# S4 convolution and SwiGLU, two layers on one core: blocks 1 to 3 of layer 0 transformed during the kernel stage

## The chip, the cores and the metric

The kernel runs on one core of a Trainium2 chip. The metric is the device time of one execution in microseconds; a profile of one execution is read beside it. The engines are called PE (matrix multiply), DVE (vector), ACT (activations), POOL (GpSimd) and SP (which issues most transfers). The matrix results land in PSUM, everything else is in SBUF or in DRAM scratch tensors.

## What is computed

x has 2048 rows of 512 channels, and two layers follow each other. A layer first adds a long convolution of the normalised rows, with a kernel K of 2048 lags per channel that is built from a diagonal state space of 128 states, and then adds a SwiGLU feed-forward network (512 to 1376 and back).

```
x = x + S4(layernorm(x)); x = x + FFN(layernorm(x))      # twice, same weights
K[d,l]  = Re sum_n C[d,n] dt[d] B[d,n] exp(dt[d] A[d,n] l)
S4(u)   = irfft(rfft(u, 2L) * rfft(K, 2L))[:L] + u * Dskip
FFN(v)  = (silu(v @ w_gate) * (v @ w_up)) @ w_down
```

## The kernel before

The sequence is cut into four blocks of 512 rows. A block's normalised rows are transformed by products with DFT matrices into eight **units**, one for each half h of the channels and each q of four groups of frequencies; a unit is a tile u of 128 x 2 x 256. Block b's output needs the units of blocks 0 to b, each multiplied by a spectrum of the convolution kernel (w0r for lag block 0, wdr in DRAM for the others), and an inverse transform. Units that are used again are kept in DRAM, in udr.

**The kernel stage** (to about 290 us) builds K for 64 channels at a time, in eight chunks. Inside `tc.manual_schedule` the order of instructions on ACT, DVE and PE is the order in which the program writes them; the transfers on SP and the work on POOL are placed by a scheduler. In pass i of the loop DVE builds the powers for chunk i + 1 (`gen_g`, `gen_e`) and the turns for chunk i + 2 (`gen_turns`, whose first instruction, L349, opens DVE's pass); ACT computes exponentials (mu and re) and sines; PE multiplies them to lags (`lags`, pk), spreads them (`spread`, kp, which also adds d_skip from the tile dsk) and transforms them into spectra (`spectra`, pw). ACT squares the FFN weights on the way (L306, `norm_units`: three loads into buffers of tag "w", three squares, three PE products, twice in a pass) to find their scales.

Units come from two routines. `direct` (L271) makes a unit with eight fp32 products (L276), a copy from PSUM by ACT (L279) and a write to udr by SP (L280). `forward` (L230) makes the eight units of a block with additions on DVE (tiles bt and z, L216), a split into two fp16 halves by ACT and DVE, twelve fp16 products a unit (L260) and a copy by ACT (L262).

- Block 0 of layer 0: `direct`, eight units, before the loop.
- Block 1 of layer 0: its rows are normalised before the loop and written to ndr; `second` loads them (two loads of 256 KB a unit, tag "w") and makes one unit in each of passes 0 to 5, and two more behind the loop.
- Blocks 2 and 3 of layer 0, and blocks 0 to 3 of layer 1: `forward`, during the FFN stretch, after a load of the block's rows and their normalisation on ACT (`norm_x`).

A tag names a set of buffers: "w" has three, "t" and "y1" one. A tile takes the buffer of the tile before it, once that one's last reader is done. During the loop dsk lies in "t" and mz2 (the powers at the five doublings) in "y1".

**The FFN stretch** (from 345 us) alternates a block's convolution (`ssm`, mostly DVE: products L683 and sums L686, then fp16 inverse products L702 on PE) with the FFN of the block before it (`ffn`, mostly PE), in the order SEQ: layer 0's blocks 0, 1, 2, layer 1's block 0, layer 0's block 3, layer 1's blocks 1, 2, 3. A scheduler sets the order there. `inputs` hands the units out, one ahead of its use.

Of the kernel before, what the change touches and what calls it, by code (L numbers as in the profile page):

```python
# [11 lines left out]
F32 = mybir.dt.float32  # L12
# [24 lines left out]
NA = 21  # L37
TB = 256
BOOST = 1 << 20
HALF = 2  # L40
INV = 1
SEQ = ((0, 0), (0, 1), (0, 2), (1, 0), (0, 3), (1, 1), (1, 2), (1, 3))

# [29 lines left out]
def kernel(ctx, tc, x, a_re, a_im, b_re, b_im, c_re, c_im, log_dt, d_skip,  # L73
# [66 lines left out]
    G.memset(hpi, math.pi / 2)  # L140

    wdr = dram.tile([NB, 2, 4, P, 2, HD], F32, name="wdr")
    udr = [dram.tile([NB - 1, 2, 4, P, 2, HD], F32, name=f"udr{i}") for i in range(NL)]
    xdr = dram.tile([NB, 4, P, D], F32, name="xdr")
    ndr = dram.tile([2, 2, P, 2, HD], F32, name="ndr")


    e0, er_, ep = (sb.tile([P, 4], F32, name=f"e{i}") for i in range(3))
# [80 lines left out]
    def forward(n, h, eh):  # L229


        hs = slice(h * HD, (h + 1) * HD)
        x0, x1, x2, x3 = (n[:, c, hs] for c in range(4))
        bt = tl([P, 7, HD], "bt", "bt")
        a_, b_, p_, q_, r_, s_, hx = (bt[:, i] for i in range(7))
        stt(a_, x2, HH, x0, OP.add)
        stt(b_, x2, -HH, x0, OP.add)
        A.activation(hx, x2, AF.Copy, scale=HH)
        stt(p_, x3, TT, x1, OP.add)
        stt(r_, x3, -TT, x1, OP.add)  # L240
        stt(q_, x1, TT, x3, OP.subtract)
        stt(s_, x1, TT, x3, OP.add)
        for i, q in enumerate(QORD):
            z = z2[:, 0 if eh else i % 2]
# [3 lines left out]
            if eh:  # L248
                hl = z2[:, 1].bitcast(F16).rearrange("p i (l d) -> p l i d", l=2)
                A.activation(hl[:, 0], z, AF.Copy, scale=256.0)  # L250
                stt(hl[:, 1], z, 256.0, hl[:, 0], OP.subtract)
            pf = psml([P, 2, HD], "pf")
            with tc.high_priority(offset=BOOST):
                for o in range(2):
                    if eh:
                        terms = [(eh[:, q, o + i, le], hl[:, lz, i]) for i in range(2) for le, lz in ((0, 0), (0, 1), (1, 0))]
                    else:
                        terms = [(ef[:, q, o + i], z[:, i]) for i in range(2)]
                    for k, (e, m) in enumerate(terms):
                        PE.matmul(pf[:, o], lhsT=e, rhs=m, start=k == 0, stop=k == len(terms) - 1)  # L260
                u = tl([P, 2, HD], "u", "u")
                A.activation(u, pf, AF.Copy, scale=2.0 ** -16 if eh else 1.0)  # L262
            yield q, u

    def norm_early(xt, n, factors):
# [13 lines left out]
        A.activation(u, pf, AF.Copy)  # L279
        nc.sync.dma_start(udr[0][b, h, q], u)  # L280

    def second(h, q, space=psml):
        n = []
        for cp in range(2):
            t = tl([P, 2, HD], "n1", "w")
            nc.sync.dma_start(t, ndr[h, cp])
            n += [t[:, 0], t[:, 1]]
        return direct(1, h, q, n, space)


    def norms():
# [38 lines left out]
        V.tensor_scalar(sc6.bitcast(I32), bits, 23, None, OP.logical_shift_left)  # L330

    mz2 = tl([P, 2, 5, DC], "mz2", "y1")

    def gen_tiles(ch):
        re = tl([P, DC, 65], "re", f"W{2 * (ch % 2)}")
# [127 lines left out]
    def spread(ch, ks):  # L465


        kp = pbig([P, 4, 16, 16], "kp")
        for grp in range(4):
            d0 = ch * DC + 16 * grp  # L470
            for ga in range(4):
                PE.matmul(kp[32 * ga:32 * ga + 32, grp], lhsT=ident[:, 32 * grp:32 * grp + 32], rhs=ks[:, ga],
                          start=True, stop=ga > 0, tile_position=(0, 32 * ga))
            PE.matmul(kp[0:32, grp, 0], lhsT=ident[0:1, 0:32], rhs=dsk[:, d0:d0 + 16], start=False, stop=True,
                      tile_position=(0, 0))
        return kp

# [132 lines left out]

    def inputs():

        for layer, b in SEQ:
# [17 lines left out]
            if (layer, b) == SEQ[HALF]:  # L631
                eh.append(tl([P, 4, 3, 2, P], "eh", "ef", F16))
                nc.sync.dma_start(eh[0], c_eh)
            for h in range(2):
                for q, u in forward(n, h, eh[0] if eh else None):
# [210 lines left out]
    with tc.manual_schedule(engines={mybir.EngineType.Activation, mybir.EngineType.DVE, mybir.EngineType.PE}):  # L846
# [35 lines left out]
        take(fw[3], 1)  # L882
        for h in range(2):
            for cp in range(2):
                nc.sync.dma_start(ndr[h, cp], x1[:, 2 * cp:2 * cp + 2, h * HD:(h + 1) * HD])
        for f in fw[4:6]:
            take(tr, 1)
            take(f, 1)
# [5 lines left out]
        take(ex, 13)  # L894
        take(fw[7], 1)
        kt2 = tl([P, 2, 4, 16, 16], "kt2", "xf")
        sec = [(h, q) for h in range(2) for q in QORD]
        sp = iter(())
        for i in range(NCH - 1):
            pk = lags(ts[i], gs[i])  # L900
            more = i + 2 < NCH
            tn = rd = f = iter(())
            if more:
                ts[i + 2] = gen_tiles(i + 2)
                tn = gen_turns(i + 2, ts[i + 2])
            gs[i + 1] = tl([P, 2, DC, 32], "g", ("gb", "ga")[i % 2])
            gg, ge = gen_g(i + 1, ts[i + 1], gs[i + 1]), gen_e(ts[i + 1])
            take(ex, 100)
            take(sp, 2)
# [24 lines left out]
            while tops:  # L934
                tops.pop(0)()
            take(sp, 1)
            kp = spread(i, ks)
            if more:
                f = second(*sec[i])
                next(f)  # L940
            take(gg, 1)
            take(rd, 1)
            take(gg, 1)
            take(rd, 3)
            if more:
                tr = gen_trig(ts[i + 2])
                take(tr, 1)
            kt = kt2[:, i % 2]
            A.activation(kt, kp, AF.Copy)
            take(tr, 1)  # L950
            take(f, 1)
            take(tr, 1)
            take(gg, 1)
            if more:
                sp = spectra(i, kt, 0, NB)
                take(sp, 1)
                ex = gen_exp(i + 2, ts[i + 2])
                take(ex, 9)
                norm_units(3, 9)
                take(ex, 4)  # L960
                take(sp, 2)
                norm_units(0, 0)
                take(ex, 14)
                take(sp, 2)
                sizes(i, kt, ks)
                take(ge, 2)
                take(gg, 1)
                take(ge, 2)
                while tops:
                    tops.pop(0)()  # L970
                ts[i] = gs[i] = None
            else:
                sizes(i, kt, ks)
                take(ge, 2)
                take(gg, 1)
                take(ge, 2)
# [8 lines left out]
        xs, eh = [None] * 3, []  # L985
        spec, ahead = inputs(), []
        first = ssm(0, 0)
        sp = spectra(i, kt, 0, NB, QORD[:3])
# [45 lines left out]
        take(pscale, 1)  # L1034
        take(first, 2)
        take(rest, 2)
        take(second(*sec[-2], space=pbig), 2)
# [6 lines left out]
        take(second(*sec[-1], space=pbig), 2)  # L1044
        take(rest, 100)
        split(1, 0)
        take(first, 1)
# [48 lines left out]
```

## Time and profile before

| | us |
|---|---|
| median of 3 runs (1209.34 to 1214.46) | 1213.57 |
| the profiled execution, span | 1210.1 |
| PE busy | 1104.0 |
| DVE busy | 1048.5 |
| ACT busy | 646.3 |
| POOL busy | 187.8 |
| the passes of the loop, on DVE | 31.05, 33.86, 34.13, 33.87, 34.14, 32.92, 29.50 |
| end of the last pass to the first FFN matmul | 56.8 |
| FFN stretch, 345 us to the end | 865 |

A row of the view by stages gives a stretch, its length, and the busy time of each engine with its number of instructions; PEclk is the share of full clock that TensorE was granted. A row of the timeline gives start and length in us, engine, line, operation, output <- inputs, shapes and count, and in brackets the idle time of the engine before it and what ended it. A row of the view by lines ends with busy us, mean ns of one | idle time before. Shapes of matmuls are weights, then moving data; an fp32 product stands as two records. A row of transfers ends with KB each and the median us from issue to landing.

### The profile page before, as it was taken

The numbers are of one execution on the slowest core, as the hardware profiler recorded it, in microseconds if no ns is written. First come the engines' busy times: TensorE is split into PE (matmuls) and PEld (weight loads), VectorE is DVE, ScalarE is ACT, GpSimd is POOL, SyncE is SP. The second block draws the span as 40 slices with busy tenths as digits, with TensorE's granted clock in tenths as the row PEclk, the third lists the DMA queues.
The fourth block names the chain that finished last, engine by engine and source line by source line (L and its number), as shares of the span: only waits on it lengthen the run. The fifth ranks groups of instructions, "written<-read, shape, count | busy, mean of one in ns | idle before, by whom it ended". The sixth has DMA issues, their size and how long they took to land.

```text
span 1210.1 us, 25368 instructions
## 1 busy us (share of the span) xinstructions
PE 1104.0 (91%) x10220; PEld 858.5 (71%) x10220; DVE 1048.5 (87%) x1677; ACT 646.3 (53%) x1392; POOL 187.8 (16%) x209
## 2 busy tenths in 40 slices
PE   3877988888978998989999999999999999999998
PEld 2755766666976776868686777778686776867875
DVE  8999999999869999999998999999992799983221
ACT  7999999973265545526753524664431553324111
POOL 1116343453220010101100000121000010000000
PEclk9999998889999999999999999999999999999999
DMA  6223233236389427433245353424433144311000
GB/s 226 96 88 92 72 89 86 73 107 184 116 285 264 127 67 199 133 118 88 62 157 140 105 179 133 125 79 146 140 118 129 33 119 132 117 58 44 14 23 18
DMA packets 134857, 138.66 MB, mean 115 GB/s; under 512 B 75921, under 2 KB 85137, under 8 KB 134738
## 3 DMA queue, kind: packets, MB, share of 16 engines
q1 hardware_dynamic: 132178, 128.64, 35.4%
q0 software_dynamic: 2560, 8.39, 2.0%
q8 instruction: 80, 1.31, 0.5%
q14 instruction: 39, 0.32, 0.1%
HBM read 98.71 MB, written 28.31 MB: 105 GB/s over the span
## 4 chain that ended last, share of the span: by engine, by line
DVE 32%; PE 27%; issue 5%; DMA 4%; ACT 2%; POOL 2%; SPq 1%; DVEq 0%; ACTq 0%; POOLq 0%
DVE t L683 5%; PE pgu L807 5%; PE pgu L808 5%; PE pgu L809 5%; DVE yk L686 4%; DVE z L216 3%; DVE yk L683 3%; PE py L821 3%; PE py L822 3%; PE py L823 3%; PE pi L702 2%; DVE sg L813 2%; DVE hl L815 1%; DVE yl L216 1%; DVE bt L216 1%
## 5 line engine op out<-in xcount | busy, mean ns | idle before, releaser
L807 PE MATMUL pgu<-mix,wsl 128*128 128x256 f16 x1280 | 350.5, 274 | 7.9 <-DVE sg L813 4.4
L809 PE MATMUL pgu<-mix,wsl 128*128 128x256 f16 x1280 | 350.5, 274 | 1.2 <-DVE wsl L579 1.2
L808 PE MATMUL pgu<-mix,wsl 128*128 128x256 f16 x1280 | 350.4, 274 | 0.0
L808 PEld LDWEIGHTS <-wsl 128*128 128x128 f16 x1280 | 125.8, 98 | 24.6 <-issue 8.6
L821 PE MATMUL py<-wsl,hh 128*128 128x512 f16 (+1 forms) x352 | 134.6, 382 | 9.3 <-DVE xg L826 5.3
L809 PEld LDWEIGHTS <-wsl 128*128 128x128 f16 x1280 | 125.8, 98 | 16.5 <-DVE wsl L579 1.5
L807 PEld LDWEIGHTS <-wsl 128*128 128x128 f16 x1280 | 125.8, 98 | 15.8
L823 PE MATMUL py<-wsl,hl 128*128 128x512 f16 (+1 forms) x352 | 134.4, 382 | 2.4 <-DVE hl L815 2.4
L812 ACT ACTIVATE sg<-pgu,sc 128x512 f32<-128x512 f32 x80 | 54.5, 682 | 128.8 <-PE pgu L809 110.9
L822 PE MATMUL py<-wsl,hh 128*128 128x512 f16 x320 | 122.1, 382 | 0.0
L683 DVE TENSOR_TENSOR t<-uu,w 128x1024 f32<-128x1024 f32 x96 | 116.8, 1217 | 5.5 <-DMA uu<-udr 5.3
L686 DVE TENSOR_TENSOR yk<-yk,t 128x1024 f32<-128x1024 f32 x96 | 116.7, 1215 | 0.1
L493 PE MATMUL pw<-kt,ek 128*128 128x256 f32 (+2 forms) x420 | 105.4, 392 | 0.0
L813 DVE SCALAR_TENSOR_TENSOR sg<-pgu,sc,sg 128x512 f32<-128x512 f32 x80 | 59.6, 744 | 52.3 <-ACT sg L812 52.0
L702 PE MATMUL pi<-yl,mix 128*128 128x256 f16 x672 | 91.4, 273 | 5.5 <-ACT yl L691 3.5
L493 PEld LDWEIGHTS pw<-kt,ek 128*128 128x128 f32 x420 | 83.9, 208 | 11.9
L814 ACT ACTIVATE hh<-sg 128x512 f16<-128x512 f32 x80 | 50.0, 626 | 67.6 <-DVE sg L813 67.6
L211 POOL TENSOR_TENSOR rs<-mv,mhalf 128x2 f32<-128x2 f32 (+1 forms) x21 | 38.7, 1845 | 275.7 <-ACT mv L210 275.6
L260 PE MATMUL pf<-z,eh 128*128 128x256 f16 x576 | 74.4, 272 | 1.6 <-ACT z L250 1.6
L702 PEld LDWEIGHTS <-mix 128*128 128x128 f16 x672 | 65.3, 98 | 14.3 <-issue 3.9
L691 ACT ACTIVATE yl<-mix,sy 128x512 f16<-128x512 f32 x56 | 40.2, 717 | 61.4 <-DVE mix L688 61.2
L504 POOL COPY w0r<-s 128x128 f32<-128x128 f32 x29 | 48.1, 1659 | 141.7 <-ACT s L502 122.2
(221 smaller groups left out, 2292.0 us busy)
## 6 DMA issues: line engine op xcount, KB each, us to landing
w<-wdr SPq DMA_DIRECT2D x96, 256.0 KB, 2.8
uu<-udr SPq DMA_DIRECT2D x96, 256.0 KB, 3.0
udr<-u POOLq DMA_DIRECT2D x32, 256.0 KB, 2.8
wdr<-wo SPq DMA_DIRECT2D x96, 64.0 KB, 2.0
udr<-u SPq DMA_DIRECT2D x16, 256.0 KB, 2.5
n<-ndr SPq DMA_DIRECT2D x16, 256.0 KB, 3.0
n<-xdr SPq DMA_DIRECT2D x4, 1024.0 KB, 6.0
xg<-in_A_u_dram SPq DMA_DIRECT2D x3, 1024.0 KB, 7.4
```

What stands on the lines that cost most here:

```text
L260: PE.matmul(pf[:, o], lhsT=e, rhs=m, start=k == 0, stop=k == len(terms) - 1)
L493: PE.matmul(pw[:, i], lhsT=e, rhs=kt[:, :, c + 4 * k0:4 * k1:4, :].rearrange("p g k d -> p k g d"), start=c == 0, stop=c == 3)
L683: V.tensor_tensor(t, uu.unsqueeze(1).to_broadcast([P, 2, 2, HD]), w.unsqueeze(2).to_broadcast([P, 2, 2, HD]), OP.mult)
L686: V.tensor_tensor(yk, yk, t, OP.add)
L702: PE.matmul(pi[:, o], lhsT=e, rhs=m, start=k == 0, stop=k == len(terms) - 1)
L807: PE.matmul(o, lhsT=wgu(wi, k, 0)[:, fs], rhs=nh[:, k], start=k == 0, stop=False)
L808: PE.matmul(o, lhsT=wgu(wi, k, 0)[:, fs], rhs=nlo[:, k], start=False, stop=False)
L809: PE.matmul(o, lhsT=wgu(wi, k, 1)[:, fs], rhs=nh[:, k], start=False, stop=k == 3)
L813: V.scalar_tensor_tensor(sg, pgu[:, 1], sc6[:, 4:5], sg, OP.mult, OP.mult)
L821: PE.matmul(py[:, r], lhsT=hh[:n, f, rc], rhs=wd(f, 0)[:n], start=f == 0, stop=False)
L822: PE.matmul(py[:, r], lhsT=hh[:n, f, rc], rhs=wd(f, 1)[:n], start=False, stop=False)
L823: PE.matmul(py[:, r], lhsT=hl[:n, f, rc], rhs=wd(f, 0)[:n], start=False, stop=f == FT - 1)
```

## The change

Blocks 1 to 3 of layer 0 are now all made by `direct` during the kernel stage, 24 units instead of 8.

- `early_row(b, c)` loads 128 rows of x into a tile xr2 (tag "w"), takes bn_stats and bn_aggr on DVE, the reciprocal root on POOL (two operations), scales on DVE and writes to ndr. Blocks 2 and 3 have eight such rows; two are done in each of passes 0 to 3.
- `later()` hands out the 24 units in order. For each block and half it loads one tile n1 of 512 KB into tag "t", which four units read.
- A pass makes three units (fa behind the lags, f behind kp, fc between two spectra), the last pass four (fa, f and two more behind f); the last two follow behind the loop as before.
- `forward` keeps only its fp16 form, and layer 0 does not use it. `inputs` loads the units of layer 0's blocks from udr. That removes two blocks of `norm_x` and `forward` from the FFN stretch; 8 writes of units from POOL's queue go too.
- Since n1 takes "t", d_skip is loaded in two halves, into the end of a tile mzd that also holds mz2, and into wx.

```diff
-    dsk = tl([1, D], "dsk", "t")
-    nc.sync.dma_start(dsk, d_skip)
+    mzd = tl([P, 4 * HD], "mzd", "y1")
+    mz2 = mzd[:, :2 * 5 * DC].rearrange("p (k l d) -> p k l d", k=2, l=5)
+    dsk = mzd[0:1, 3 * HD:], wx.bitcast(F32)[0:1]
...
+    def early_row(b, c):
+
+        xr = tl([P, D], "xr2", "w")
+        nc.sync.dma_start(xr, x[0, b * T + c * P:b * T + (c + 1) * P, :])
+        row = tl([P, 16], "row", "stats")
+        st, mv, rs = row[:, :6], row[:, 6:8], row[:, 8:9]
+        V.bn_stats(st, xr)
+        V.bn_aggr(mv, st)
+        G.tensor_scalar(rs, mv[:, 1:2], EPS, 1.0, OP.add, OP.mult)
+        G.tensor_tensor(rs, rs, mhalf[:, 0:1], OP.pow)
+        yield
+        V.tensor_scalar(xr, xr, mv[:, 0:1], rs, OP.subtract, OP.mult)
+        nc.sync.dma_start(ndr[b - 1, :, :, c].rearrange("h p d -> p h d"), xr.rearrange("p (h d) -> p h d", h=2))
+
+    def later():
+
+        for b in range(1, NB):
+            for h in range(2):
+                n = tl([P, 4, HD], "n1", "t")
+                nc.sync.dma_start(n, ndr[b - 1, h])
+                for q in QORD:
+                    yield lambda space=psml, b=b, h=h, q=q, n=n: direct(b, h, q, [n[:, c] for c in range(4)], space)
...
-            if layer == 0 and b < 2:
+            if layer == 0:
...
             norm_units(0, 0)
+            fa = next(sec)()
+            next(fa)
             ks = spread_in(pk)
             take(gg, 1)
             take(tn, 1)
+            early = [early_row(*rows.pop(0)) for _ in range(2)] if rows else []
+            for e in early:
+                take(e, 1)
             take(gg, 1)
             take(tn, 1)
             if more:
                 rd = gen_reduce(ts[i + 2])
                 next(rd)
+            take(fa, 1)
+            for e in early:
+                take(e, 1)
...
             kp = spread(i, ks)
-            if more:
-                f = second(*sec[i])
-                next(f)
+            f = next(sec)()
+            next(f)
...
                 norm_units(3, 9)
+                fc = next(sec)()
+                next(fc)
                 take(ex, 4)
                 take(sp, 2)
                 norm_units(0, 0)
+                take(fc, 1)
...
             else:
+                fb = [next(sec)() for _ in range(2)]
+                for fc in fb:
+                    next(fc)
                 sizes(i, kt, ks)
+                for fc in fb:
+                    take(fc, 1)
```

Three places show how instructions stand now. The first is DVE at the start of pass 3; t is the tile of turns, xr a tile of `gen_turns` or, with a number, the row of x. Before:

```order
L424 TENSOR_TENSOR xi<-xi,mz_154 128x320
L349 TENSOR_TENSOR t_1792<-am,th 128x1024
L427 TENSOR_TENSOR g<-w_151,re 128x128
L428 TENSOR_TENSOR tmp<-w_151,im 128x128
L352 TENSOR_TENSOR xi<-am,th 128x320
L430 TENSOR_TENSOR g<-g,tmp 128x64
```

and in the change:

```order
L360 TENSOR_TENSOR t_1912<-am,th 128x1024
L286 BN_STATS row<-xr_1983 128x6
L287 BN_AGGR row<-row 128x2
L286 BN_STATS row<-xr_1990 128x6
L287 BN_AGGR row<-row 128x2
L438 TENSOR_TENSOR g<-w_151,re 128x128
L439 TENSOR_TENSOR tmp<-w_151,im 128x128
L363 TENSOR_TENSOR xi<-am,th 128x320
L291 TENSOR_SCALAR xr_1983<-xr_1983,row 128x512
L291 TENSOR_SCALAR xr_1990<-xr_1990,row 128x512
L441 TENSOR_TENSOR g<-g,tmp 128x64
```

The statistics of both rows stand right behind the instruction that opens the pass (now L360), and both scalings three instructions later.

The second is SP at the same boundary; st is a piece of a weight, u a unit. Before:

```order
L304 DMA st<-in_B_w_gate_dram 128x344 x3
L516 DMA wdr<-wo 256x1x64 x6
L286 DMA n_1921<-ndr 128x512
L286 DMA n_1923<-ndr 128x512
L304 DMA st<-in_B_w_gate_dram 128x344
```

and in the change:

```order
L317 DMA st<-in_B_w_gate_dram 128x344 x3
L278 DMA udr_114<-u 128x512
L527 DMA wdr<-wo 256x1x64 x6
L283 DMA xr_1983<-in_A_u_dram 128x512
L283 DMA xr_1990<-in_A_u_dram 128x512
L317 DMA st<-in_B_w_gate_dram 128x344
L527 DMA wdr<-wo 256x1x64 x3
L292 DMA ndr<-xr_1983 128x2x256
L292 DMA ndr<-xr_1990 128x2x256
```

The two row loads stand where the two loads of n stood. In the built program the first of them waits for the square of the first of the three st above, the second for that of the second, as the loads of n did.

The third is PE in the last pass, from kp on. Before:

```order
L474 MATMUL kp<-dsk,ident 32x16
L493 MATMUL pw<-kt_489,ef 128x256
L493 MATMUL pw<-kt_489,ek_83 128x256 x3
L493 MATMUL pw<-kt_489,ef 128x256
L493 MATMUL pw<-kt_489,ek_83 128x256 x3
```

and in the change:

```order
L485 MATMUL kp<-wx,ident 32x16
L274 MATMUL pf<-n_2909,ef 128x256
L274 MATMUL pf<-n_2909,ek_84 128x256 x3
L274 MATMUL pf<-n_2909,ef 128x256
L274 MATMUL pf<-n_2909,ek_84 128x256 x3
L274 MATMUL pf<-n_3336,ef 128x256
L274 MATMUL pf<-n_3336,ek_83 128x256 x3
L274 MATMUL pf<-n_3336,ef 128x256
L274 MATMUL pf<-n_3336,ek_83 128x256 x3
L274 MATMUL pf<-n_3336,ef 128x256
L274 MATMUL pf<-n_3336,ek_84 128x256 x3
L504 MATMUL pw<-kt_489,ef 128x256
```

Three units stand between kp and the first spectrum (a fourth ahead of kp), and the second of them begins a new tile n.

More of the change, by code (lines that the diff above doesn't have):

```diff
@@ L39 @@
 BOOST = 1 << 20
-HALF = 2
 INV = 1
@@ L142 @@
     wdr = dram.tile([NB, 2, 4, P, 2, HD], F32, name="wdr")
-    udr = [dram.tile([NB - 1, 2, 4, P, 2, HD], F32, name=f"udr{i}") for i in range(NL)]
+    udr = [dram.tile([NB - i, 2, 4, P, 2, HD], F32, name=f"udr{i}") for i in range(NL)]
     xdr = dram.tile([NB, 4, P, D], F32, name="xdr")
-    ndr = dram.tile([2, 2, P, 2, HD], F32, name="ndr")
+    ndr = dram.tile([NB - 1, 2, P, 4, HD], F32, name="ndr")
     e0, er_, ep = (sb.tile([P, 4], F32, name=f"e{i}") for i in range(3))
@@ L177, in gen_w @@
         V.tensor_tensor(w0[:, 1], w0[:, 1], wt[:, 1], OP.add)
-    dsk = tl([1, D], "dsk", "t")
-    nc.sync.dma_start(dsk, d_skip)
+    mzd = tl([P, 4 * HD], "mzd", "y1")
+    mz2 = mzd[:, :2 * 5 * DC].rearrange("p (k l d) -> p k l d", k=2, l=5)
+    dsk = mzd[0:1, 3 * HD:], wx.bitcast(F32)[0:1]
+    for i in range(2):
+        nc.sync.dma_start(dsk[i], d_skip[:, i * HD:(i + 1) * HD])
     def stats(src, rows, scale, tag="stats", between=None):
@@ L243, in forward @@
         for i, q in enumerate(QORD):
-            z = z2[:, 0 if eh else i % 2]
+            z = z2[:, 0]
             u_, v_ = ((p_, a_) if q in (0, 3) else (q_, b_))
@@ L247, in forward @@
             stt(z[:, 1], s_ if q in (0, 3) else r_, CC, hx, OP.add if q < 2 else OP.subtract)
[L248 to L251, printed above, removed]
+            hl = z2[:, 1].bitcast(F16).rearrange("p i (l d) -> p l i d", l=2)
+            A.activation(hl[:, 0], z, AF.Copy, scale=256.0)
+            stt(hl[:, 1], z, 256.0, hl[:, 0], OP.subtract)
             pf = psml([P, 2, HD], "pf")
@@ L254, in forward @@
                 for o in range(2):
[L255 to L258, printed above, removed]
+                    terms = [(eh[:, q, o + i, le], hl[:, lz, i]) for i in range(2) for le, lz in ((0, 0), (0, 1), (1, 0))]
                     for k, (e, m) in enumerate(terms):
@@ L261, in forward @@
                 u = tl([P, 2, HD], "u", "u")
[L262 removed]
+                A.activation(u, pf, AF.Copy, scale=2.0 ** -16)
             yield q, u
@@ L280, in direct @@
         nc.sync.dma_start(udr[0][b, h, q], u)
[L282 to L288, printed above, removed]
+    def early_row(b, c):
[17 more added lines that the diff above has]
+                    yield lambda space=psml, b=b, h=h, q=q, n=n: direct(b, h, q, [n[:, c] for c in range(4)], space)
     def norms():
@@ L473, in spread @@
                           start=True, stop=ga > 0, tile_position=(0, 32 * ga))
-            PE.matmul(kp[0:32, grp, 0], lhsT=ident[0:1, 0:32], rhs=dsk[:, d0:d0 + 16], start=False, stop=True,
+            PE.matmul(kp[0:32, grp, 0], lhsT=ident[0:1, 0:32], rhs=dsk[d0 // HD][:, d0 % HD:d0 % HD + 16], start=False, stop=True,
                       tile_position=(0, 0))
@@ L611, in inputs @@
     def inputs():
+        eh = []
         for layer, b in SEQ:
-            if layer == 0 and b < 2:
+            if layer == 0:
                 if b == 0:
@@ L630, in inputs @@
             norm_x(n)
-            if (layer, b) == SEQ[HALF]:
+            if not eh:
                 eh.append(tl([P, 4, 3, 2, P], "eh", "ef", F16))
@@ L634, in inputs @@
             for h in range(2):
-                for q, u in forward(n, h, eh[0] if eh else None):
+                for q, u in forward(n, h, eh[0]):
                     if b < NB - 1:
@@ L884 @@
             for cp in range(2):
-                nc.sync.dma_start(ndr[h, cp], x1[:, 2 * cp:2 * cp + 2, h * HD:(h + 1) * HD])
+                nc.sync.dma_start(ndr[0, h, :, 2 * cp:2 * cp + 2], x1[:, 2 * cp:2 * cp + 2, h * HD:(h + 1) * HD])
         for f in fw[4:6]:
@@ L896 @@
         kt2 = tl([P, 2, 4, 16, 16], "kt2", "xf")
-        sec = [(h, q) for h in range(2) for q in QORD]
+        sec = later()
+        rows = [(b, c) for b in range(2, NB) for c in range(4)]
         sp = iter(())
@@ L984 @@
         nc.sync.dma_start(ei, c_ei)
-        xs, eh = [None] * 3, []
+        xs = [None] * 3
         spec, ahead = inputs(), []
@@ L1036 @@
         take(rest, 2)
-        take(second(*sec[-2], space=pbig), 2)
+        take(next(sec)(pbig), 2)
         take(first, 1)
@@ L1043 @@
         take(rest, 3)
-        take(second(*sec[-1], space=pbig), 2)
+        take(next(sec)(pbig), 2)
         take(rest, 100)
```

1 line of the change is left out of this document (removed).

## Prediction

> **What bounds the kernel now.** I read the busy time by stage first. The stages are the seven passes of the chunk loop (each from one DVE instruction L349 to the next), the stretch to the first FFN matmul at 345 us, and the FFN stretch in three pieces.
>
> ```profile
> span 1210.1 us, 25368 instructions
> core 0: us, PE busy (x) PEld busy (x) DVE busy (x) ACT busy (x) POOL busy (x), PEclk, DMA share, GB/s
> ...
> 191.64:225.78 34.14, 28.75 (x384) 22.46 (x382) 34.07 (x47) 31.02 (x83) 10.81 (x15) 0.90 0.28 79
> ...
> 258.70:288.20 29.50, 25.20 (x445) 19.84 (x446) 29.22 (x38) 13.45 (x39) 16.25 (x14) 0.99 0.44 127
> 288.20:345.00 56.80, 50.42 (x474) 44.11 (x463) 47.11 (x93) 18.13 (x29) 18.84 (x27) 0.97 0.60 179
> 345.00:600.00 255.00, 234.83 (x1969) 181.67 (x1968) 243.23 (x418) 139.88 (x264) 26.36 (x30) 0.98 0.50 147
> 600.00:900.00 300.00, 291.68 (x2470) 229.31 (x2469) 294.26 (x479) 140.49 (x270) 25.98 (x29) 0.99 0.43 131
> 900.00:1210.10 310.10, 301.41 (x2478) 226.33 (x2476) 182.55 (x282) 97.60 (x183) 7.94 (x11) 1.00 0.23 70
> ```
>
> In a chunk DVE is busy 34.07 of 34.14 us: DVE alone sets its length, and whatever is put on DVE there, or makes it wait, is paid in full. PE is idle 5.4 us of that chunk. In the stretch to 345 us PE has most work (50.4 of 56.8). From 345 to 900 us DVE and PE are both nearly full (537 and 527 of 555), and in the last 310 us PE alone (301).
>
> The second reading is one chunk boundary, in time, on three engines.
>
> ```profile
> 155.36 1.59 DVE L416 TENSOR_TENSOR re<-re,mu 128x992 f32<-128x992 f32 x1
> 157.77 1.63 DVE L349 TENSOR_TENSOR t<-am,th 128x1024 f32<-128x1024 f32 x1
> 159.32 0.79 DVE L427 TENSOR_TENSOR g<-w,re 128x128 f32<-128x128 f32 x1
> 160.03 0.38 DVE L428 TENSOR_TENSOR tmp<-w,im 128x128 f32<-128x128 f32 x1
> 160.33 0.47 DVE L352 TENSOR_TENSOR xi<-am,th 128x320 f32<-128x320 f32 x1
> ...
> 157.83 2.94 ACT L394 ACTIVATE mu<-rho 128x64 f32<-128x64 f32 x19
> 162.59 1.23 ACT L306 ACTIVATE sq<-st 128x344 bf16<-128x344 f32 x3
> ...
> 163.09 0.81 SPq L286 DMA_DIRECT2D n<-ndr  x2
> ...
> n<-ndr SPq DMA_DIRECT2D x16, 256.0 KB, 3.0
> ...
> L279 ACT ACTIVATE u<-pf 128x512 f32<-128x512 f32 x16 | 9.2, 582 | 3.8 <-PE pf L276 3.8
> ```
>
> The loads into the three "w" buffers are issued at 163.09, 5.3 us after L349: SP holds them until ACT has squared (162.59) what the buffer held. Landing takes 3.0 us more, so such a load is usable 8.3 us after L349 starts. That is harmless today, since PE asks for it only at 168.7.
>
> **The new rows on DVE (11.2 us).** Eight x rows are normalised in chunks 0 to 3, two per chunk. The same three operations exist today:
>
> ```profile
> L192 DVE BATCH_NORM_STATS2 st<-x 128x6 f32<-128x512 f32 x4 | 2.7, 667 | 0.0
> L193 DVE BATCH_NORM_AGGREGATE mv<-st 128x2 f32<-128x6 f32 x10 | 1.8, 181 | 0.3
> L268 DVE TENSOR_SCALAR xne<-xne,rs 128x512 f32<-128x512 f32 x4 | 1.9, 543 | 0.0
> 331.66 0.78 POOL L194 TENSOR_SCALAR rs<-mv 128x2 f32<-128x2 f32 x1 [1.99 <-DVE mv L193]
> 332.53 1.30 POOL L195 TENSOR_TENSOR rs<-rs,mhalf 128x2 f32<-128x2 f32 x1
> ```
>
> 0.667 + 0.181 + 0.543 = 1.39 us a row, 11.1 to 11.2 us for eight, with no cover on a full engine.
>
> **The wait for the rows (29.6 us).** The row load stands in SP's order exactly where the ndr loads stood, takes the same "w" buffers and waits for the same squares, but its reader is DVE's bn_stats, the instruction right behind L349. DVE asks 1.6 us after L349 starts (157.77 to 159.32). ACT also gets one more copy of a unit (L279's 0.58 us) ahead of its squares, so the load lands at about 8.9 us: a wait of 7.4 us in each of four chunks, 29.6 us. Queued behind bn_stats is the whole of DVE's chunk, and for it wait ACT's sine work and PE's next lags. Could a slower DVE let ACT run ahead and end the wait? Hardly: ACT's mu tile is still being read by DVE's L416, which ends at 156.95. If ACT started right there, the square would end 0.9 us sooner and the wait be about 6 us. So the bounds are 24 and 34 us (6 and 8.5 a chunk); I take 7.4.
>
> **The wait for POOL (6 us).** rs comes from two POOL operations, 2.2 us for one row by the rows above (331.66 to 333.83), one row after the other. The first row's rs is ready 2.2 us after its aggregate, the second's 2.1 us later, or 4.3; DVE has bn_stats and aggregate of row two (0.85) and L427, L428, L352 (1.4) to do meanwhile, then the first scaling (0.5): 2.75 us. Wait 1.6 us a chunk, 6 us in four; bounds 0 (POOL finishing both within the cover) and 9. DVE's extra in chunks 0 to 3 is then 11.2 + 29.6 + 6 = 47 us.
>
> **Two more units on PE per chunk (1 us).** One unit's records today:
>
> ```profile
> 168.67 0.70 PE L276 MATMUL pf<-n,ef 128*128 128x256 f32 x2
> 169.21 1.46 PE L276 MATMUL pf<-n,ek 128*128 128x256 f32 x6
> 170.50 0.59 PE L276 MATMUL pf<-n,ef 128*128 128x256 f32 x2
> 170.93 1.46 PE L276 MATMUL pf<-n,ek 128*128 128x256 f32 x6
> ...
> 184.96 1.21 PE L310 MATMUL nrm<-sq,onesb 128*128 128x344 bf16 x3 [5.01 <-ACT sq L306]
> 185.96 1.06 PE L493 MATMUL pw<-kt,ef 128*128 128x256 f32 x2
> 186.81 2.77 PE L493 MATMUL pw<-kt,ek 128*128 128x256 f32 x6
> ```
>
> Sixteen records from 168.67 to 172.39, less the last one's tail, are 3.47 us. Two more units are 6.9 us; with today's 28.75 us that makes 35.7, but 2.5 us of those come from records at half the pace (185.96 on: 1.06 for what took 0.59) behind the 5.01 us idle, which the units fill. So PE needs 33 to 36 us. In chunks 0 to 3, now 45 us long, that is hidden. In chunks 4 and 5 it equals DVE's 33 to 34 us; DVE needs a chunk's lags only by way of ACT's later steps, so a microsecond or two of lateness stays off DVE. I charge 1 us, with bounds −2 and +6. The 16 added copies on ACT, 9 us, lie in ACT's idle 3 us a chunk. SP issues 8 row loads, 8 ndr writes and 16 udr writes more, and 6 loads of n1 for 16; at 0.4 us each (two in 0.81 us) that is some 9 us over seven chunks, and nothing of it stands ahead of a row load but the six wdr writes that stand there today.
>
> **The last pass of the loop (16 us).** There the order puts four units where there was none, three in a row behind kp.
>
> ```profile
> 274.23 0.70 PE L493 MATMUL pw<-kt,ef 128*128 128x256 f32 x2 [1.11 <-ACT kt L949]
> ...
> 287.19 0.33 PE L456 MATMUL pk<-re,g 128*32 128x64 f32 x7 [1.30 <-DVE re L416]
> ...
> st<-in_B_w_gate_dram SPq DMA_DIRECT2D x3, 688.0 KB, 4.7
> ```
>
> Between 258.7 and the last lags PE waited 1.11 and 1.30 us, 2.4 in all, which is what four units (13.9 us) can hide behind. The third unit also opens a new 512 KB tile in the single "t" buffer, whose load can only be issued when the second unit's matmuls are done; between 3.0 us (256 KB) and 4.7 us (688 KB) I take 4. 13.9 + 4 − 2.4 = 15.5, with a little lateness from chunk 5, 16 us. Behind the lags stand kp, the spectra and the first FFN matmul, in PE's order, in a stretch that PE fills 89%, so I pass it on whole; bounds 8 (half taken up by the waits in that stretch) and 20.
>
> [...]
>
> **What the FFN stretch gets back (30 us).** Blocks 2 and 3 of layer 0 lose their forward transform: of six such blocks today, two.
>
> ```profile
> L216 DVE SCALAR_TENSOR_TENSOR z<-bt 128x256 f32<-128x256 f32 x96 | 36.3, 416 | 0.1
> L216 DVE SCALAR_TENSOR_TENSOR z<-z 128x512 f16<-128x512 f32 x48 | 32.8, 683 | 2.1 <-ACT z L250 2.1
> L216 DVE SCALAR_TENSOR_TENSOR bt<-n 128x256 f32<-128x256 f32 x72 | 25.5, 416 | 1.4 <-ACT n L227 1.4
> L260 PE MATMUL pf<-z,eh 128*128 128x256 f16 x576 | 74.4, 272 | 1.6 <-ACT z L250 1.6
> 655.61 1.47 PE L260 MATMUL pf<-z,eh 128*128 128x256 f16 x12
> 656.92 0.27 PE L809 MATMUL pgu<-mix,wsl 128*128 128x256 f16 x1
> ```
>
> PE loses 192 of 576 records, and twelve take 1.31 us (655.61 to 656.92): 21 us. DVE loses a third of 36.3 + 32.8 + 25.5, or 32 us. Where PE alone is the bound the gain is 21; where DVE is, 32. Up to 900 us PE's own idle time is 28.5 us (555 − 526.5), and part of it goes as DVE gets lighter: 21 + 9 = 30, with bounds 15 (if the first removed block merely frees the engine that was not late) and 42. The u tiles that replace the work are 16 loads of 256 KB, 3 us each, issued a unit ahead and off both engines.
>
> **Sum.** +47 + 1 + 16 − 30 = +34 us on the profiled 1210.1, so 1244; the median of the runs lies 3.5 us above that execution (1213.57), so 1247.
>
> **Rivals.** Less wait, a faster kernel: if the row loads landed before DVE asks, 29.6 and most of the 6 us would go. Then 11 + 1 + 1 + 16 − 30 = −1, and with the last pass at 8 and the gain at 42, −21: 1193 to 1213. It decides from the point where the square ends 2 us ahead of L349 (0.4 for the issue and 3.0 for the landing, less the 1.6 at which DVE asks). For it: ACT is not the bound. Against it: ACT's mu must wait for DVE's L416, and the squares stand behind it. I give 0.10, of which 0.07 for more than 0.5% faster (0.5% being about what a measurement here can tell from no change) and 0.03 within.
> The gain stays out: if between 345 and 900 us it is transfers and the ACT and POOL steps of the norms that hold the engines, only 15 us return, and the last pass costs 20: 47 + 1 + 20 − 15 = +53, 1267. The full DVE and PE rows speak against it, the 0.50 DMA share for it: 0.15.
> The gain is larger: the stretch is DVE's, 42 us return and the last pass is half hidden: 47 + 1 + 8 − 42 = +14, 1228. For it, DVE's 243 of 255 us; against it, the last 310 us, which are PE's: 0.15.
>
> **How the numbers follow.** The forecast, 1247 with 1236 to 1258 of its own, has 0.60. Its neighbours at 1228 and 1267 bring in 0.30, so 1222 to 1266 should hold eight in ten. Faster 0.07, within 0.5% 0.04 (0.03 from the rival, 0.01 from the lower neighbour's tail), slower 0.89.
>
> **What would show it.** In the new profile bn_stats should stand with an idle time before it of 6 to 8.5 us in four chunks, put down to the row load, and those chunks be about 45 us long, chunks 4 and 5 34 to 36. The second scaling should wait for POOL. The last lags should come about 43 us after the lags before it, not 27, and the first FFN matmul near 409 us, not 345. From there to the end should be about 835 us, not 865. I am wrong if DVE stays full in chunks 0 to 3, if the units leave the last pass its length, or if the FFN stretch does not shrink.

## The result, and the profile after

The changed kernel takes 1251.39 us (median of 4 runs, 1243.76 to 1254.04), the kernel before beside it 1214.01. The ratio is 1.029, with a 95% interval of 1.024 to 1.035: slower by 2.4 to 3.5%. The profiled execution took 1252.3 us, 42.2 us more than the profiled one of before (1210.1). Each kernel's time below is the median of its fast runs: of the kernel with the rows later one run is left out (1328.09 us, at a granted clock of 0.85), and of the one without rows three (1222.94 us and more, over 1.5% above its fastest).

The first part of the page of the changed kernel gives, for each engine, its busy time, the share of the span and the count of instructions.

```profile
span 1252.3 us, 25438 instructions
PE 1135.0 (91%) x10284; PEld 888.7 (71%) x10284; DVE 1023.1 (82%) x1627; ACT 618.3 (49%) x1330; POOL 192.7 (15%) x215
```

The busy time by stage shows where the 42 us lie. The stretches are passes 0 to 3, pass 4, from pass 5's start on DVE to the start of PE's lags before last, from there to the last lags, from there to the first FFN product, and the FFN stretch; the columns are length, busy time of PE, PEld, DVE, ACT and POOL (with counts), PE's granted clock, and the DMA's share and rate.

```profile
58.66:236.11 177.45, 139.63 (x1662) 110.67 (x1657) 137.02 (x208) 129.48 (x332) 72.88 (x64) 0.91 0.32 94
236.11:269.94 33.83, 32.30 (x414) 26.45 (x407) 33.76 (x48) 31.97 (x84) 19.67 (x15) 1.00 0.29 80
269.94:315.25 45.31, 33.33 (x370) 27.03 (x359) 35.41 (x52) 32.54 (x85) 21.92 (x15) 0.89 0.29 79
315.25:362.26 47.01, 39.51 (x433) 31.83 (x432) 32.12 (x48) 14.46 (x42) 11.55 (x15) 0.93 0.51 150
362.26:419.30 57.04, 52.02 (x531) 46.03 (x531) 40.95 (x75) 18.72 (x30) 16.17 (x25) 0.94 0.47 136
419.30:1252.30 833.00, 804.88 (x6721) 617.88 (x6719) 691.16 (x1102) 341.61 (x639) 42.82 (x60) 0.99 0.39 118
```

Before, DVE was busy all through a pass. In passes 0 to 3 it is now busy 137 of 177 us: 40 us of these four passes are a DVE that waits. In the third row, pass 5, PE is idle for 12 us and DVE for 10, and in the last pass of the loop DVE is idle for 15 while PE works at a granted clock of 0.93. The same stages for all kernels of this study, worked out from the same markers in each trace (us):

| kernel | to pass 0 | passes 0–3 | pass 4 | pass 5 to lags before last | to last lags | to first FFN product | FFN stretch | span |
|---|---|---|---|---|---|---|---|---|
| before | 58.7 | 132.9 | 34.1 | 34.5 | 26.9 | 57.8 | 865.1 | 1210.1 |
| after | 58.7 | 177.5 | 33.8 | 45.3 | 47.0 | 57.0 | 833.0 | 1252.3 |
| rows later | 58.5 | 154.1 | 33.9 | 46.7 | 46.0 | 56.3 | 830.4 | 1225.8 |
| tiles from ACT | 59.1 | 169.9 | 33.8 | 33.5 | 42.3 | 56.8 | 830.5 | 1225.9 |
| both edits | 59.0 | 139.8 | 34.9 | 39.8 | 38.6 | 54.6 | 841.1 | 1207.8 |
| half units | 58.2 | 177.0 | 33.8 | 43.1 | 39.2 | 55.4 | 829.3 | 1236.1 |
| two blocks | 58.4 | 136.7 | 33.8 | 33.6 | 27.9 | 53.3 | 845.4 | 1189.2 |
| FFN only | 58.7 | 137.2 | 33.9 | 35.2 | 26.1 | 57.3 | 835.0 | 1183.4 |
| no rows | 58.5 | 137.2 | 33.9 | 51.7 | 45.3 | 54.5 | 831.2 | 1212.3 |
| no rows, tiles from ACT | 58.3 | 135.4 | 33.9 | 35.0 | 39.4 | 55.9 | 841.1 | 1198.9 |

So of the +42.2: +44.6 in passes 0 to 3, +10.8 in pass 5, +20.1 in the last pass, −1.1 in pass 4 and behind the last lags, −32.1 in the FFN stretch.

The same view of the kernel before, for its passes 0 to 3, pass 5 and the last pass:

```profile
58.73:191.64 132.91, 110.13 (x1438) 84.41 (x1429) 132.51 (x184) 125.58 (x325) 55.39 (x49) 0.91 0.29 82
...
225.78:260.29 34.51, 29.33 (x384) 22.26 (x382) 34.44 (x47) 32.19 (x92) 20.11 (x16) 0.90 0.33 88
260.29:287.19 26.90, 22.60 (x368) 17.75 (x368) 26.62 (x35) 11.86 (x30) 13.74 (x11) 1.00 0.44 129
```

DVE's busy time in passes 0 to 3 has grown by only 4.5 us (132.5 to 137.0), though eight rows were added; its other operations took some 7 us less than before. The one that begins a pass is an example: 1.63 us in the row that the prediction shows, 1.21 us below.

DVE's waits in the kernel stage (58 to 360 us) of the changed kernel: who waited for whom, us in total, times, the longest.

```profile
DVE row L286 <- DMA xr<-in_A_u_dram: 39.2, 4, 16.1
DVE cmx L326 <- PE nrm L323: 13.4, 2, 9.8
```

And the groups of the row steps and of the units' products. The last columns are busy time and mean ns of one, then the idle time of the engine before them and who ended most of it.

```profile
L286 DVE BATCH_NORM_STATS2 row<-xr 128x6 f32<-128x512 f32 x8 | 5.5, 684 | 39.3 <-DMA xr<-in_A_u_dram 39.2
L291 DVE TENSOR_SCALAR xr<-xr,row 128x512 f32<-128x512 f32 x8 | 4.3, 544 | 0.6 <-POOL row L289 0.4
L287 DVE BATCH_NORM_AGGREGATE row<-row 128x2 f32<-128x6 f32 x8 | 1.5, 182 | 0.3
L289 POOL TENSOR_TENSOR row<-row,mhalf 128x1 f32<-128x1 f32 x8 | 5.1, 634 | 0.7
L274 PE MATMUL pf<-n,ef 128*128 128x256 f32 x96 | 32.3, 421 | 32.9 <-DMA n<-ndr 32.9
```

Two waits stand out: 39.2 us of DVE for the rows, and 32.9 us of PE for the 512 KB tiles of normalised rows (n), which have one buffer. The second is no bystander. This is the end of pass 2 and the start of pass 3 in time (start, duration, engine), on SP, ACT and DVE: the longest wait for a row.

```profile
176.55 1.85 SPq L527 DMA_DIRECT2D wdr<-wo  x3
178.44 0.61 SPq L299 DMA_DIRECT2D n<-ndr  x1
...
188.62 0.60 ACT L277 ACTIVATE u<-pf 128x512 f32<-128x512 f32 x1 [9.31 <-PE pf L274]
...
198.89 1.23 ACT L319 ACTIVATE sq<-st 128x344 bf16<-128x344 f32 x3
...
199.38 0.90 SPq L283 DMA_DIRECT2D xr<-in_A_u_dram  x2
...
184.76 1.21 DVE L360 TENSOR_TENSOR t<-am,th 128x1024 f32<-128x1024 f32 x1
202.12 0.70 DVE L286 BATCH_NORM_STATS2 row<-xr 128x6 f32<-128x512 f32 x1 [16.15 <-DMA xr<-in_A_u_dram]
```

The load of the tile stands in SP's order behind wdr writes, is issued at 178.44 and holds PE until 183 us; ACT waits 9.31 us for the unit's product to copy it, so its squares, which free the rows' buffers, run at 198.89, the row load is issued at 199.38, and DVE, ready at 186, starts at 202.12. The other three passes wait 7.4 to 8.0 us, as forecast.

### The profile page after: what moved, and what is told of

It is laid out like the page before. It is cut to its first block, busy times and chain, and to the rows that moved or that the text cites. A ratio compares the mean times of both kernels' runs of the same rounds, so it can differ in the third digit from the quotient of the medians.

```text
span 1252.3 us, 25438 instructions
## 1 busy us (share of the span) xinstructions
PE 1135.0 (91%) x10284; PEld 888.7 (71%) x10284; DVE 1023.1 (82%) x1627; ACT 618.3 (49%) x1330; POOL 192.7 (15%) x215
## 4 chain that ended last, share of the span: by engine, by line
PE 35%; DVE 20%; issue 8%; DMA 3%; ACT 2%; POOL 1%; SPq 0%; DVEq 0%; POOLq 0%; ACTq 0%
PE pgu L819 6%; PE pgu L820 6%; PE pgu L821 6%; PE py L833 4%; PE py L834 3%; PE py L835 3%; DVE t L695 3%; PE pi L714 3%; DVE yk L698 2%; PE pf L258 2%; DVE yk L695 2%; DMA mix<-nn 2%; DVE z L218 1%; DVE sg L825 1%; DVE hl L827 1%
## 5 line engine op out<-in xcount | busy, mean ns | idle before, releaser
L824 ACT ACTIVATE sg<-pgu,sc 128x512 f32<-128x512 f32 x80 | 54.6, 682 | 139.2 <-PE pgu L821 136.0
L714 PE MATMUL pi<-yl,mix 128*128 128x256 f16 x672 | 93.8, 277 | 10.5 <-ACT yl L703 7.1
L504 PE MATMUL pw<-kt,ek 128*128 128x256 f32 (+2 forms) x420 | 100.9, 380 | 0.0
L515 POOL COPY w0r<-s 128x128 f32<-128x128 f32 x29 | 67.8, 2338 | 178.7 <-ACT s L513 178.7
L504 PEld LDWEIGHTS pw<-kt,ek 128*128 128x128 f32 x420 | 80.7, 200 | 10.4
L274 PE MATMUL pf<-n,ek 128*128 128x256 f32 x288 | 75.7, 402 | 0.0
L695 DVE TENSOR_TENSOR yk<-u,w0r 128x1024 f32<-128x1024 f32 x56 | 68.3, 1220 | 0.1
```

The source lines that it names most:

```text
L274: PE.matmul(pf[:, i], lhsT=e, rhs=n[c], start=c == 0, stop=c == 3)
L504: PE.matmul(pw[:, i], lhsT=e, rhs=kt[:, :, c + 4 * k0:4 * k1:4, :].rearrange("p g k d -> p k g d"), start=c == 0, stop=c == 3)
L695: V.tensor_tensor(t, uu.unsqueeze(1).to_broadcast([P, 2, 2, HD]), w.unsqueeze(2).to_broadcast([P, 2, 2, HD]), OP.mult)
L714: PE.matmul(pi[:, o], lhsT=e, rhs=m, start=k == 0, stop=k == len(terms) - 1)
```

## The experiments

All were run beside the kernel before; each ratio is against it. Theory 1 throughout: the loss is waits for loads (rows on DVE, tiles on PE) plus the units from pass 5 on. Theory 2, the rival: the 55 us or so of added products on PE set the length, and the waits are their shadow.

**Rows later.** DVE's row steps move behind work that it has anyway; the loads stay.

```
         nc.sync.dma_start(xr, x[0, b * T + c * P:b * T + (c + 1) * P, :])
+        yield
...
             take(fa, 1)
-            for e in early:
-                take(e, 1)
...
+            for e in early:          # behind four pairs of gg and ge
+                take(e, 1)
...
+            for e in early:          # behind three pairs of gg and rd
+                take(e, 1)
```

> The row loads stay where they are, but DVE's bn_stats and bn_aggr of both rows stand behind the first four steps of the g and e tables and the scalings behind three more, so some 12 us of DVE's own work lie between the first reduction of a pass and the first use of a row. Theory 1 (DVE pays for the landing of the row loads): the idle time before bn_stats, 39.2 us in four passes of the changed kernel, falls below 5; passes 0 to 3 go from 41.4, 42.8, 41.9 and 51.4 us to 34 to 37; the time falls by 28 to 38 us, to 1213 to 1223. Theory 2 (the products of the added units fill PE, and DVE's wait is only the shadow of that): the wait moves to another DVE instruction and the passes stay over 40 us; the time falls by less than 10 us.

1222.32 us, ratio 1.0046 (1.0012 to 1.0081): 29.1 us less than the changed kernel, the near end of theory 1. The groups of waits of this run from 58 to 360 us:

```profile
DVE cmx L327 <- PE nrm L324: 21.6, 3, 11.1
...
DVE row L287 <- DMA xr<-in_A_u_dram: 3.9, 2, 2.2
```

The wait for rows is gone (3.9 us of 39.2), but passes 1 to 3 are still 41.9, 40.4 and 38.0 us long, not 34 to 37. A part went elsewhere, as theory 2 said: DVE now waits 21.6 us for nrm, a product of PE that stands in PE's order behind units. In passes 1 and 2 the cause is not theory 2's, since PE is not full there (33.06 of 41.90 us, 32.13 of 40.40). Only in pass 3 is it (37.86 of 38.00), with more records than either of the two passes before:

```profile
92.30:134.20 41.90, 33.06 (x372) 26.57 (x363) 34.95 (x54) 31.41 (x82) 13.69 (x18) 0.88 0.36 106
134.20:174.60 40.40, 32.13 (x397) 25.65 (x397) 36.37 (x53) 30.37 (x78) 15.26 (x18) 0.87 0.36 98
174.60:212.60 38.00, 37.86 (x442) 31.12 (x441) 35.93 (x54) 34.83 (x93) 12.14 (x18) 1.00 0.41 118
```

In pass 1 the trace shows what PE waits for, and how fast it works afterwards:

```profile
115.32 1.19 PE L274 MATMUL pf<-n,ef 128*128 128x256 f32 x2 [7.36 <-DMA n<-ndr]
116.31 2.77 PE L274 MATMUL pf<-n,ek 128*128 128x256 f32 x6
118.87 1.06 PE L274 MATMUL pf<-n,ef 128*128 128x256 f32 x2
```

7.36 us for the tile, and then records at half pace (six in 2.77 us; 1.46 is their usual time).

**Tiles from ACT's queue.** The next tile is loaded behind the copy of the last unit that read the one before; the last tile goes into a buffer (tag "z") that is free by then.

```
+        if then:
+            then()           # behind the u copy on ACT
...
-                nc.sync.dma_start(n, ndr[b - 1, h])
+            queue.dma_start(ns[-1], ndr[b - 1, h])   # queue: ACT; SP for the first and last
```

> Each 512 KB tile of normalised rows but the first and the last is loaded from ACT's queue, issued right behind the copy of the last unit that read the tile before it, and so not behind the wdr and udr writes in SP's order; the last tile goes into another buffer, which is free in the last pass, and is loaded at that pass's start. Nothing else changes. Theory 1 (the loads' lateness is paid by PE): the waits of 11.6, 10.5 and 6.1 us in passes 2, 5 and 6 fall below 2 each; pass 3's wait for its rows goes from 16.2 to about 7.5 us; the lags before last come 10 to 15 us earlier against their pass's start, the last lags 6 to 9 us nearer to them; the time falls by 20 to 30 us, to 1221 to 1231. Theory 2 (PE's products are the bound there): PE only does later work sooner and waits elsewhere; less than 8 us.

1227.63 us, ratio 1.0107 (1.0066 to 1.0148): 23.8 us less than the changed kernel. PE's waits for tiles, 32.9 us before, fall to 1.3 and 0.5 us, and with them pass 3's wait for its rows falls from 16.2 us to 6.7 and 1.7. Pass 3 goes from 51.4 to 43.5 us, pass 5 to the lags before last from 45.3 to 33.5 (the whole loss), the last pass from 47.0 to 42.3, a little less than expected. The tile of pass 5 comes from ACT's queue, that of the last pass has a buffer of its own. Pass 5 up to the lags in this run:

```profile
262.70:296.30 33.60, 31.68 (x372) 25.83 (x362) 33.53 (x46) 32.02 (x84) 23.21 (x16) 1.00 0.41 119
```

**Both.**

> The two edits together. Theory 1: the two waits are separate but for pass 3, where some 8.5 us are counted in both, so 50 to 60 us fall away: 1190 to 1202, faster than the kernel before by 1 to 2%. Theory 2: PE, which needs 33 to 36 us in each of six passes with three units, sets the length: less than 25 us fall away, and the kernel stays slower than before.

1210.32 us, ratio 0.9962 (0.9936 to 0.9988). That is 41 us less than the changed kernel and no longer slower than before, but 9 us short of the 50 to 60 expected, between the two theories' windows. Its busy times by stage, from pass 5 to the last lags:

```profile
233.60:273.40 39.80, 36.58 (x426) 29.69 (x424) 35.97 (x52) 35.33 (x91) 12.50 (x16) 0.96 0.37 107
273.40:312.10 38.70, 36.35 (x436) 29.88 (x437) 32.17 (x48) 14.47 (x42) 11.34 (x15) 1.00 0.55 169
```

The second row is the last pass: once the waits are gone PE is busy 36.4 of 38.7 us at a granted clock of 1.00, and theory 2 holds there. Pass 5 takes 39.8 us, where the run with tiles from ACT alone took 33.5. PE has 426 records to do in it against that run's 372, so with shorter passes it reaches pass 5 with work left over. The FFN stretch takes 841.1 us, against 829 to 833 in the five kernels with three blocks that reach it later, at 381 to 419 us; the run without rows that loads its tiles from ACT's queue reaches it at 358 us and takes 841.1 too. Yet the run with the FFN part only reaches it at 348 us and takes 835.0, so why the stretch is longer here no run settles.

**Half units.** Each unit leaves out the products of chunks 2 and 3.

```
-            for c in range(4):
+            for c in range(2):
```

> Each of the 24 units leaves out its products for the chunks 2 and 3 (eight of sixteen records), so PE does 1.73 us less per unit, 42 us in all; loads, copies and rows stay. Theory 1: in passes 0 to 4 that is hidden (PE waits for DVE there), and only the units from pass 5 on count, nine of them, 8 to 16 us; the waits for the rows and for the tiles stay as they are: 1235 to 1243. Theory 2 (PE throughput is the cost): nearly all of the 42 us falls away, to 1209 to 1216.

1236.23 us, ratio 1.0161 (1.0120 to 1.0201): 15 us less than the changed kernel, where 42 us of products were taken out. PE's waits for tiles stay (34.0 us against 32.9), and passes 0 to 4 keep their length (177.0 and 33.8), pass 5 loses 2.2, the last pass 7.8, near the 6.9 of its four halved units. The halved products cost nothing in passes 0 to 4, where DVE waits for rows; in the last pass they cost their full time.

**Two blocks.** Both edits, and block 3 keeps its forward transform in the FFN stretch: 16 units and 4 rows in place of 24 and 8.

```
-        todo = [(b, h) for b in range(1, NB) for h in range(2)]
+        todo = [(b, h) for b in range(1, NB - 1) for h in range(2)]
...
-            if layer == 0:
+            if layer == 0 and b < NB - 1:
```

> The two edits of the run before (rows used later, tiles loaded from ACT's queue), and block 3 of layer 0 goes back to the FFN stretch: 16 units in passes 0 to 5 instead of 24, 4 rows instead of 8, none in the last pass nor behind it. Theory 1 (from pass 5 on PE sets the end, each unit there costs its 3.47 us): against the run with both edits the last pass loses 11 to 12 us, the stretch behind it 7, pass 5 some 5, DVE 5.6 us of rows; the FFN stretch grows by 10 to 16 us; in sum 1192 to 1202, faster than before by 1 to 1.8%. Theory 2 (DVE is what the first half of the FFN stretch waits for, and a kernel stage that ends sooner on PE gives DVE no lead there): the FFN stretch grows by 20 us or more, and the time stays between 1205 and 1213.

1200.31 us, ratio 0.9879 (0.9846 to 0.9911): the fastest kernel here that leaves nothing out, 1.2% faster than before. The last stages:

```profile
228.90:262.50 33.60, 28.68 (x324) 21.82 (x313) 33.53 (x46) 31.98 (x87) 23.45 (x17) 0.90 0.28 76
262.50:290.50 28.00, 22.61 (x372) 17.73 (x373) 27.73 (x36) 11.95 (x34) 13.47 (x12) 1.00 0.45 130
290.50:343.80 53.30, 44.71 (x499) 39.58 (x498) 44.23 (x88) 15.61 (x22) 16.72 (x24) 0.94 0.54 164
343.80:1189.20 845.40, 815.96 (x6817) 627.50 (x6815) 707.88 (x1145) 361.36 (x684) 49.80 (x64) 0.99 0.38 115
```

DVE fills pass 5 and the last pass again (33.5 of 33.6, 27.7 of 28.0), and the FFN stretch is only 4 us longer than with both edits and three blocks. The time is the one that theory 1 forecast, but its parts are not: the stretch behind the last lags lost 1.3 us and not 7, and the FFN stretch grew by 4.3 and not by 10 to 16. In the profiled executions block 3 cost 23 us of kernel stage (366.7 against 343.8 us at the first FFN product) and gave 4 us back. But the profiled execution with two blocks (1190.98 us) was the fastest of its six runs, 9 us below their median. By the medians the two kernels are 10.0 us apart and not 18.6, so an estimate of what block 3 gives back in most runs is nearer to 13 us than to 4.

**FFN only.** The kernel before, with blocks 2 and 3 of layer 0 taking block 1's transformed values.

```
-            if layer == 0 and b < 2:
+            if layer == 0:
...
-                            nc.sync.dma_start(u, udr[0][b, h, q])
+                            nc.sync.dma_start(u, udr[0][min(b, 1), h, q])
```

> The kernel before, with its kernel stage untouched, but blocks 2 and 3 of layer 0 take block 1's transformed values instead of computing their own forward transform: the changed kernel's FFN stretch without its kernel stage. Theory 1 (the 32 us that the stretch lost are the removed work): the FFN stretch goes from 865 to 831 to 836 us, the time to 1180 to 1186. Theory 2 (part of them came because the late last pass let DVE and ACT run ahead before the first FFN product): the stretch keeps 840 us or more, the time is 1189 to 1197.

1186.75 us, ratio 0.9784 (0.9753 to 0.9815); the FFN stretch is 835.0 us, 30.1 less than before. The gain there is the removed work; no late kernel stage is needed for it (theory 1), though the median lies 0.75 us above its window.

**No rows, and no rows with tiles from ACT.** The eight rows are loaded and written as they are; the second run loads the tiles from ACT's queue too.

```
-        V.bn_stats(st, xr)
-        V.bn_aggr(mv, st)
-        G.tensor_scalar(rs, mv[:, 1:2], EPS, 1.0, OP.add, OP.mult)
-        G.tensor_tensor(rs, rs, mhalf[:, 0:1], OP.pow)
...
-        V.tensor_scalar(xr, xr, mv[:, 0:1], rs, OP.subtract, OP.mult)
```

> The changed kernel without the normalisation of the eight rows: each row is loaded and written to ndr as it is, so bn_stats, bn_aggr, the two POOL operations and the scaling are gone (the later blocks are transformed unnormalised). Theory 1 (rows cost DVE their 11 us in full besides the wait): 11 us below the run in which they stand later, 1209 to 1214. Theory 2 (once DVE doesn't wait for rows, the late 512 KB tiles set passes 1 to 3, by way of the norms' products behind them on PE): the passes stay at 38 to 42 us as in that run, and the time is 1216 to 1224.

1213.90 us, ratio 0.9992 (0.9954 to 1.0030): the upper end of theory 1's window, though its runs spread from 1204.86 to 1221.99 us. Passes 1 to 3 are 37.8, 33.3 and 35.5 us long and not 38 to 42, which speaks against theory 2. But the way there is not theory 1's either. Passes 0 to 3 are 16.9 us shorter than with the rows later (137.2 against 154.1), and PE still waits for tiles, 23.6 us in all and 14.5 of it in pass 5:

```profile
PE pf L274 <- DMA n<-ndr: 23.6, 4, 14.5
```

Some of the gain is lost again in pass 5 (51.7 us against 46.7), so the rows' work cannot be read from this run alone. Hence the second one:

> The run with both edits, without the normalisation of the eight rows (each is loaded and written to ndr as it is; the later blocks are transformed unnormalised): what the rows' own work costs once neither they nor the tiles are waited for. Theory 1 (11 us of DVE, in full): passes 0 to 3 go from 33.7, 35.6, 35.2 and 35.4 us to 31 to 33, and the time from 1210 to 1197 to 1202. Theory 2 (with three units a pass PE is by then as full as DVE, 33 to 36 us): the passes stay at 33 to 35 us, the time at 1204 to 1211.

1204.51 us, ratio 0.9930 (0.9906 to 0.9954): the lower edge of theory 2's window, and passes 0 to 3 are 33.9 us long in the mean, inside its 33 to 35. The time is 5.8 us by the medians, and 8.9 by the profiled executions, below the run with both edits; passes 0 to 3 are 4.4 us shorter. Of the rows' 11.3 us of DVE work half to four fifths are paid, not all.

## Why the prediction was right, and where its terms were off

The sign, the mechanism and the range held (1247 predicted, 1251.4 measured). By its own steps:

- **Rows' work**, 11.2 us: measured 8 × (684 + 182 + 544) ns = 11.3 us on DVE. With the waits gone it is worth 6 to 9 us of time. In the run without rows PE is busy 128.1 of the 135.4 us of passes 0 to 3, and DVE 132.7; that this is why not all of it is paid is argued, not shown.
- **Wait for the rows**, 4 × 7.4 = 29.6 with bounds 24 to 34: 39.2, above the bounds. Three passes had 7.64, 8.04 and 7.38; pass 3 had 16.15. The step named what the row load waits for (the squares), and ran those squares at a fixed distance from the pass's start. It did not ask what could hold ACT ahead of them: a copy of a unit whose tile was late. With the tiles loaded from ACT's queue pass 3 waited 8.4 us.
- **Wait for POOL**, 6 us: 0.6. The cost was taken from operations on 128x2 (2.2 us for the pair); on 128x1 they take 0.34 + 0.63 us, inside the cover.
- **Two more units per pass**, 1 us with bounds −2 to +6: +10.8 in pass 5. This is the step that failed. It counted PE's busy time and put the wait for the single tile buffer into the last pass alone. The same buffer changes hands in passes 1, 2, 4 and 5 as well; in passes 1, 2 and 5 PE waited 4.7, 11.6 and 10.5 us for it. In pass 5 that held ACT's copy by 10.97 us and DVE's reduction of nrm by 9.8. Loading the tiles from ACT's queue brought pass 5 back to 33.5 us.
- **The last pass**, 16 us: 20.1. Its units were sized right: in the run with both edits, where the wait is gone, the pass is 38.6 us, 11.7 longer than before, against 13.9 − 2.4 = 11.5. The wait was 6.1 us and not 4, and behind it 16 records took 6.5 us (340.80 to 347.32) where 3.5 are usual:

```profile
340.80 1.19 PE L274 MATMUL pf<-n,ef 128*128 128x256 f32 x2 [6.08 <-DMA n<-ndr]
341.78 2.77 PE L274 MATMUL pf<-n,ek 128*128 128x256 f32 x6
344.34 1.06 PE L274 MATMUL pf<-n,ef 128*128 128x256 f32 x2
345.19 2.29 PE L274 MATMUL pf<-n,ek 128*128 128x256 f32 x6
347.32 0.59 PE L274 MATMUL pf<-n,ef 128*128 128x256 f32 x2
```

Behind the wait the trace shows slower records, at about half the usual pace at first: six take 2.77 us and then 2.29 where 1.46 is usual, and some 3 us are lost after 6.08 us idle. The slow records do not always last as long, 6.5 us here and 3.5 us in pass 5 (295.72 to 299.18) after 10.45 us idle; what sets that, no run shows. The prediction read such records in the kernel before (1.06 us for what took 0.59, behind 5.01 us idle), but its sum has no term for them behind the wait of this pass. The granted clock of the pass is 0.93 in the changed kernel, 0.96 with the tiles from ACT's queue and 1.00 with both edits.

- **FFN stretch**, −30, of which 21 PE's own work and 9 its idle time: −32.1, with 23.0 us less PE work (827.9 to 804.9) and 9.1 us less idle time. With the change's FFN part alone it is −30.1, with 26.1 and 4.0: the total is firm, how it divides is not.

The sum missed by 8.5 us (42.3 by the stages, against 33.8 before it was rounded to 34). Too low were the wait for the rows by 9.6, pass 5 by 9.8 and the last pass by 4.1; too high were the wait for POOL by 5.4 and the FFN stretch by 2.1; pass 4 and the stretch behind the last lags came 1.1 shorter; and some 6.5 us in passes 0 to 3 came back by DVE's other operations, which took less time there, for a reason that no run here shows. So errors of some 24 and 15 us in opposite directions partly cancel. The medians lie only 4.4 us apart, since the 3.5 us that the forecast added from the profiled execution to the median came as −0.9. The runs show the main waits that were forecast; that 1247 lies so near to 1251.4 is in part luck.

Of the markers, the FFN stretch (about 835, came 833.0), the four waits before bn_stats but for pass 3's size, and passes of about 45 us held (44.4 in the mean, though three were 41 to 43 and pass 3 51.4); pass 5, the last lags (43 us behind the lags before them, came 47), the first FFN product (409, came 419) and POOL's wait did not. The rival with a faster kernel was out for the changed kernel; its condition, rows that land before DVE asks, was made true in the run with the rows later, which came to 1222.3 us and not to its 1193 to 1213. Only with the tiles in time as well did the time fall into that range (1210.3).

## What to carry to other kernels

When a change adds a load into a buffer that exists once, list every place where that buffer changes hands, and at each ask what is queued behind the waiting engine: here one late tile stopped PE (10.45 us in pass 5), and through PE's order ACT's copy (10.97) and DVE's reduction (9.8); in pass 3 another held up, through ACT, the row loads (16.15 us of DVE's wait). Put the first use of a loaded tile behind work that the engine has anyway, and issue the load from the queue that already waits for the buffer's last reader. Move work out of a stage only as far as the receiving stage has idle time on that engine: the second block's transform found it in the passes, the third block's did not, and left the kernel 10 us slower by the medians.

## What the runs showed of the hardware

The same 512 KB load landed in a median 4.5 us from SP's queue in the changed kernel and in 3.3 us from ACT's queue (the sixth part of the two pages: issues, KB of each, median us to landing):

```profile
n<-ndr SPq DMA_DIRECT2D x6, 512.0 KB, 4.5
```

```profile
n<-ndr ACTq DMA_DIRECT2D x4, 512.0 KB, 3.3
n<-ndr SPq DMA_DIRECT2D x2, 512.0 KB, 3.6
```

Whether that is the queue or the moment of issue stays open: the two loads left on SP's queue landed in 3.6 us in the same run. POOL's power took 634 ns on one column in the mean of the changed kernel's eight records. The record on two columns that the prediction took has 1.30 us, but 19 records of the changed kernel on two and four columns range from 0.70 to 3.03 us, so no price per column follows from these runs.
